# A two-headed attention kernel: input turned by DMA, queries ahead of keys, windowed values made once per token

## The chip, the cores and the metric

The kernel runs on one core of one Trainium2 chip. The metric is the device time of one execution in microseconds; the times shown are those of five executions, and one more view, the profile, comes from one of these five. In the profile's pages PE is TensorE (its weight loads, PEld, are counted apart), ACT is ScalarE, DVE is VectorE, POOL is GpSimd and SP is SyncE, which here only issues DMAs.

## The reference

Two attention blocks with inputs of their own are computed, and their results are laid side by side in the last dimension. Both have 2048 tokens, a width of 448 and 16 heads of 28.

```python
# A: one key head and one value head shared by 16 query heads, every token sees every token
q = (x @ wq).reshape(B, S, 16, 28)      # k = x @ wk, v = x @ wv: 28 columns each
p = softmax(q k^T * 28**-0.5)           # 2048 x 2048 for each head
a = (p @ v).reshape(B, S, 448) @ wo
# B: own keys and values for each head; a token sees 8 tokens: itself, and 2, 4 .. 14 back
q, k, v = split(x @ wqkv)
b = (softmax over those 8) @ v ... @ wo
return concatenate([a, b], axis=-1)
```

A is by far the larger part: 16 x 2048 x 2048 exponentials.

## The kernel before

**A planner writes the order.** `_Gen` runs a small model of the five engines while the program is being built. Each engine has a clock in it (`T`); `loop` takes the engine whose clock is lowest and lets it choose its next step. The order in which steps were chosen is the order in which each engine's instructions stand in the program. Waits on semaphores follow from what each operation reads and writes (`Res`, `emission`). An engine executes its list strictly in order, so a plan that is wrong about a duration shows as a wait in front of whatever stands next. DMA issues stand in the list of the engine that issues them: nearly all on SP, some at the start on ACT, and the weights of B and of the two output projections on POOL.

**Block A.** Scores are made in jobs of 128 keys by 512 queries for one head. A query group is 4 heads by 512 queries (`Group`: 16 key blocks by 4 heads, 64 jobs), and 16 such groups make 1024 jobs. `do_qk` (L1426) issues two or three jobs at once into PSUM banks 0 to 2 or 3 and 4 in turn, and `act_choose` (L1192) takes the exponential of two or three banks with one ACT instruction into one of 8 buffers of `P`. A part of the jobs, called D jobs, does not go through ACT: `dread` makes their exponentials on DVE (L1473), as bit patterns with an offset, with two shifted copies (L1481, L1488, on DVE or POOL), and four small products per job against scaled copies of the values in place of one. `want_d` decides when such a job may be added: among other things the number of finished fills (`nfill`) has to keep up with `FILLN` per 1024 jobs plus `FILL0`, and before 40 us no fill of `x` or `k` may be open. Products with values (`do_pv`, L1536) collect a whole query group in one PSUM bank, four heads at a time.

**Fills.** All else on TensorE is a fill: projections of x into keys, values and queries, norms of the queries, the whole of block B, and the output projections (`outproj`). A fill has a due time and sometimes a condition; `fill_pick` takes the most overdue that can run, `pe_choose` puts it between score jobs where there is room. `dummy` (L1619, L1621) adds products with no use when a running measure of activity falls below `HAMLOW`; `step_ready` holds narrow steps of B back while it is below `HAMTILE`. Both are meant to keep the granted clock up.

**Start of A.** x arrives as 16 blocks of 128 tokens in `xn`, which lies in the upper part of `P`, so only `XFREE` buffers of `P` are free until the last block is turned. Each 512 tokens are transposed on TensorE (L666, four blocks by four pieces of 112 columns, `KA`), and evicted by DVE (L677) or ACT (L675) to `xT_A`. Then come the keys `k0` (L691, evicted at L699), the first query group (L796) with its square on ACT (L825), its copy (L815), a column sum and an addition (L747): a per-query offset that replaces the row maximum. Keys of later chunks and later query groups follow as fills. For B, x is transposed by DMAs on SP (`load_xb`, one after every second exponential).

**Block B.** A token's window reaches at most 14 back, in steps of 2, so even and odd tokens are apart: 4 chunks of 512 tokens, each cut into 21 (`NB`) blocks of 25 queries with 32 keys. Values are projected block by block (L850), 21 products of 4 chunks each, with 7 tokens of each block computed again in the next one, and evicted to `vB` (L857), which has the tokens of chunk c in partitions 32c to 32c+31. Scores (L1269), exponentials (L1290) and products with values (L1231) run for four head groups; a group may start when all values, its keys and its queries are there.

**Ends.** `chain` brings denominators through DRAM (`den`, `rec_scratch`, `bc`: three DMA steps on SP per group), multiplies on POOL (L1006), and `outproj` projects 128 tokens at a time and writes them out.

Of the kernel before, what the change touches and what calls it, by code (L numbers as in the profile page):

```python
# [5 lines left out]
ACT = mybir.ActivationFunctionType  # L6
# [6 lines left out]
S = 2048  # L13
D = 448
H = 16
DH = 28
KA = 112
# [12 lines left out]
HALO = 7  # L30

# [19 lines left out]
T0 = 13.0  # L51
AHEAD = 2
BT0 = 83
BDT = 39
# [20 lines left out]
XFREE = 3  # L75
# [3 lines left out]
HAMLOW = 0.6  # L79
HAMTILE = 0.5  # L80
# [8 lines left out]
XE1 = False  # L89
FILLN = 140.0  # L90
FILL0 = 6.0
# [98 lines left out]
class _Gen:  # L190
# [233 lines left out]
    def alloc(self, es):  # L424
# [7 lines left out]
        self.rec_dram = nc.dram_tensor("rec_scratch", (32, 4, 512), FP32)  # L432

# [42 lines left out]
        self.xn = self.P[:, self.NP * 1536 - 16 * D:].rearrange("p (b c) -> p b c", c=D)  # L476
# [7 lines left out]
    def plan_start(self):  # L484
# [20 lines left out]
        def wA(q, t, src, c1, key, lands):  # L505
            self.dma_op(q, t[0:KA, :, 0:c1], src.rearrange("(k p) c -> p k c", p=KA), writes=[res(key)], lands=lands, name=key)

        def xA(q, c, b0, b1, lands):
            self.dma_op(q, g.xn[:, 4 * c + b0:4 * c + b1, :], g.A_x[0, 512 * c:512 * c + 512, :].rearrange("(p b) c -> p b c", b=4)[:, b0:b1, :],
                        writes=[res("xn", c)] if b0 == 0 else (), appends=[res("xn", c)] if b0 else (), lands=lands, name="x")  # L510
        xA("sp", 0, 0, 2, XL0)
        xA("act", 0, 2, 4, XL0)
        wA("sp", g.wq, g.A_wq, D, "wq", 5000.0)
        wA("act", g.wk, g.A_wk, DH, "wk", 3500.0)
        wA("act", g.wv, g.A_wv, DH, "wv", 4000.0)
        for c in range(1, 4):
            xA("sp", c, 0, 4, 5000.0 + 700 * c)
        dve(lambda e: e.memset(g.zero, 0.0), 100, writes=[res("zero")])
        dve(lambda e: e.memset(g.wk[:, :, DH:32], 0.0), 80, writes=[res("wk0")])
        dve(lambda e: e.memset(g.wv[:, :, DH:32], 0.0), 80, writes=[res("wv0")])  # L520
        dve(lambda e: e.memset(g.wq[:, :, D:456], 0.0), 100, writes=[res("wq0")])
# [39 lines left out]
        gp(lambda e: e.memset(g.vB[:, :, :, DH:32], 0.0), 1400, writes=[res("vB0")])  # L561
        gp(lambda e: e.memset(g.vB[:, :, :, DH:DH + 1], 1.0), 600, reads=[res("vB0")], writes=[res("vB1")])
# [83 lines left out]
    def make_fills(self):  # L646
# [10 lines left out]
        for c in range(4):  # L657
            for kt in (range(4) if c == 0 else (0, 2)):
                n = 1 if c == 0 else 2

                def steps(bank, c=c, kt=kt, n=n):
                    out = []
                    for k in range(n):
                        for b in range(4):
                            x0 = bank * 1024 + 512 * k + 128 * b
                            out.append(("full", lambda e, b=b, k=k, x0=x0: e.transpose(g.psb[0:KA, x0:x0 + 128], g.xn[:, 4 * c + b, KA * (kt + k):KA * (kt + k) + KA],  # L666
                                                                                   g.ident[:, :]), 60.0, [res("xn", c), res("id")]))
                    return out

                def after(bank, c=c, kt=kt, n=n):  # L670
                    src = g.psb[0:KA, bank.i * 1024: bank.i * 1024 + 512 * n].rearrange("p (k t) -> p k t", k=n)
                    dst = g.xT_A[0:KA, kt:kt + n, 512 * c:512 * c + 512]
                    wr = [res("xA", c, kt + k) for k in range(n)]
                    if kt == 3 or (c == 1 and kt == 2):
# [6 lines left out]
                    if sum(self.xdone) == 16:  # L681
                        for k in range(XFREE, self.NP):
                            self.pslots.give(k)
# [164 lines left out]
        for b in range(NB):  # L848
# [5 lines left out]
            def after(bank, b=b):  # L854
                def cb(o):
                    self.vready += 1
# [872 lines left out]
```

## Time and profile before

| | us |
|---|---|
| median of five runs | 412.44 |
| lowest, highest | 410.13, 417.66 |
| the profiled execution, its span | 417.66, 415.8 |
| busy: PE, ACT, DVE, POOL | 402.7, 390.0, 349.9, 114.7 |
| exponentials of A on ACT (L1192), 352 instructions | 377.3 |
| first exponential begins | 12.15 |
| granted TensorE clock, mean | 0.974 |

The busy time of an engine covers the instructions that compute; DMA issues and waits are not in it. Busy shares are means over stages that differ: the start up to 14 us, the long middle, the B groups spread through it, and the last 14 us of output projections. The profiled execution is the longest of the five, and its clock row has a dip that the prediction comes back to.

### The profile page before, as it was taken

How to read it: one execution, taken by the hardware profiler on the slowest of the kernel's cores; microseconds unless marked ns; L12 is line 12 of the kernel's file. 1: busy time of each engine (PE TensorE's matmuls, PEld its weight loads, DVE VectorE, ACT ScalarE, POOL GpSimd, SP SyncE). 2: the span in 40 equal slices, each digit the busy share in tenths (PEclk: the TensorE clock that was granted, in tenths of full speed). 3: DMA queues.
4: the chain of work that ended last, by engine and by line, in shares of the span. 5: the costliest groups of instructions: out<-in, count | busy, mean ns of one | idle time of the engine just before them, and what ended most of it. 6: DMA issues, size and time to landing. Idle time of an engine off the chain costs nothing.

```text
span 415.8 us, 16682 instructions
## 1 busy us (share of the span) xinstructions
PE 402.7 (97%) x7348; PEld 140.9 (34%) x7348; DVE 349.9 (84%) x803; ACT 390.0 (94%) x382; POOL 114.7 (28%) x143
## 2 busy tenths in 40 slices
PE   7999999999999999999999999999999999999996
PEld 3432232322233323334324433233433223444343
DVE  2879999999999999998988998989882398599953
ACT  3899999999999999999999999999996799999972
POOL 8851051202011530404363223414121030110420
PEclk9999999999999999999999999999985699999999
DMA  7099311000010101000221102210011131102415
GB/s 220 20 208 119 68 36 28 4 5 27 2 28 2 30 24 29 6 15 21 54 62 53 29 9 67 66 19 16 6 31 32 29 82 36 43 15 76 105 56 159
DMA packets 31235, 20.15 MB, mean 48 GB/s; under 512 B 21404, under 2 KB 26316, under 8 KB 31164
## 3 DMA queue, kind: packets, MB, share of 16 engines
q1 hardware_dynamic: 29068, 16.37, 16.5%
q0 software_dynamic: 736, 2.20, 3.0%
q8 instruction: 58, 0.95, 1.0%
q10 hardware_dynamic: 1360, 0.51, 0.5%
q14 instruction: 13, 0.11, 0.1%
HBM read 12.42 MB, written 3.92 MB: 39 GB/s over the span
## 4 chain that ended last, share of the span: by engine, by line
ACT 76%; PE 21%; DMA 1%; DVE 1%; issue 0%; ACTq 0%; DVEq 0%
ACT P L1192 74%; PE ps L642 7%; PE ps L1536 6%; PE ps L1426 6%; ACT P L1290 1%; DMA wk<-in_A_wk_dram 1%; PE ps L1231 1%; PE ps L1619 1%; PE ps L1269 1%; PE ps L1259 0%; DVE qT_A L815 0%; PE ps L666 0%; DVE qT_A L747 0%; PE ps L1621 0%; DVE sq L1060 0%
## 5 line engine op out<-in xcount | busy, mean ns | idle before, releaser
L1192 ACT ACTIVATE P<-ps 128x1536 bf16<-128x1536 f32 (+1 forms) x352 | 377.3, 1253 | 7.2 <-PE ps L1426 6.9
L1473 DVE TENSOR_SCALAR Z<-ps 128x512 int16<-128x512 f32 x205 | 139.0, 683 | 15.9 <-PE ps L1426 14.8
L1536 PE MATMUL ps<-P,vA 128*32 128x512 bf16 x819 | 148.1, 394 | 1.0 <-ACT P L1192 0.5
L1426 PE MATMUL ps<-qT_A,kT_A 29*128 29x512 bf16 x1024 | 140.8, 391 | 4.1 <-ACT P L1192 1.8
L1536 PE MATMUL ps<-Z,vA 128*32 128x512 bf16 x820 | 142.9, 389 | 1.2 <-ACT P L1192 0.9
L1488 DVE TENSOR_SCALAR Z<-Z 128x1024 int16<-128x1024 int16 x174 | 77.7, 457 | 1.3
L1426 PEld LDWEIGHTS ps<-qT_A,kT_A 29*128 29x128 bf16 x1024 | 35.5, 91 | 126.8 <-ACT P L1192 65.5
L1006 POOL TENSOR_TENSOR oTn<-PVs,bc 128x512 bf16<-128x512 f32 x15 | 19.1, 1273 | 140.6 <-DVE Z L1481 83.7
L1481 DVE TENSOR_SCALAR Z<-Z 128x512 int16<-128x512 int16 x174 | 49.5, 304 | 1.0
L1536 PEld LDWEIGHTS ps<-P,vA 128*32 128x32 bf16 x819 | 36.2, 94 | 34.0 <-issue 21.3
L1536 PEld LDWEIGHTS ps<-Z,vA 128*32 128x32 bf16 x820 | 35.3, 94 | 35.2 <-issue 22.4
L1481 POOL TENSOR_SCALAR Z<-Z 128x512 int16<-128x512 int16 x31 | 19.1, 617 | 86.0 <-DVE Z L1481 31.8
L642 PE MATMUL ps<-xT_B,wB 128*32 128x512 bf16 x512 | 40.8, 391 | 0.1
L1488 POOL TENSOR_SCALAR Z<-Z 128x1024 int16<-128x1024 int16 x31 | 32.5, 1048 | 5.6 <-DVE Z L1488 3.7
L1006 POOL TENSOR_TENSOR oTnB<-PVs,bc 128x512 bf16<-128x512 f32 x16 | 20.3, 1274 | 47.1 <-DVE Z L1488 26.8
L960 DVE COPY PVs<-ps 128x512 f32<-128x512 f32 x31 | 21.2, 684 | 12.8 <-PE ps L1231 10.5
L642 PE MATMUL ps<-wB,xT_B 128*32 128x448 bf16 x336 | 24.5, 354 | 0.0
L642 PE MATMUL ps<-xT_A,wq 112*32 112x512 bf16 x256 | 20.3, 383 | 0.3 <-DVE qT_A L815 0.3
L642 PE MATMUL ps<-woA,oTn 128*32 128x448 bf16 x256 | 17.6, 356 | 0.0
L1060 DVE CAST sq<-ps 128x448 bf16<-128x448 f32 x15 | 9.2, 622 | 8.6 <-PE ps L642 8.1
L642 PEld LDWEIGHTS ps<-xT_B,wB 128*32 128x32 bf16 x512 | 10.6, 96 | 14.8 <-issue 8.9
L1231 PE MATMUL ps<-P,vB 32*32 32x25 bf16 (+1 forms) x1344 | 15.2, 173 | 0.0
(96 smaller groups left out, 271.0 us busy)
## 6 DMA issues: line engine op xcount, KB each, us to landing
bc<-rec_scratch SPq DMA_DIRECT2D x124, 64.0 KB, 2.1
out_dram<-sq SPq DMA_DIRECT2D x17, 112.0 KB, 1.8
out_dram<-ob SPq DMA_DIRECT2D x13, 112.0 KB, 1.7
P<-in_A_x_dram SPq DMA_DIRECT2D x3, 448.0 KB, 7.0
wB<-in_B_wqkv_dram POOLq DMA_DIRECT2D x1, 1008.0 KB, 6.1
den<-PVs SPq DMA_DIRECT2D x31, 8.0 KB
rec_scratch<-rec SPq DMA_DIRECT2D x31, 8.0 KB, 1.7
wq<-in_A_wq_dram SPq DMA_DIRECT2D x1, 392.0 KB, 5.5
```

What stands on the lines that cost most here:

```text
L642: ins = e.matmul(self.bank(bank, 32 * j, 32 * j + m, 0, n), lhs(j), rhs(j), start=start, stop=stop, tile_position=(0, 32 * j))
L960: return dict(emit=lambda e: e.tensor_copy(out=g.PVs[:, p, :], in_=g.bank(bank.i)), reads=[bank.res], writes=[self.pvs.res[p]], took=ns + ...
L1006: return dict(emit=lambda e: e.tensor_tensor(out=dst(z), in0=g.PVs[:, p, :], in1=g.bc[:, b, :], op=ALU.mult), reads=[self.pvs.res[p], self ...
L1060: em = lambda e: e.tensor_copy(out=self.obuf[o_], in_=g.bank(bank.i, 0, 128, 0, D))
L1192: op = self.put("act", lambda e: e.activation(g.P[:, 1536 * k:1536 * k + 512 * n], g.ps[:, lo:lo + 512 * n], ACT.Exp, scale=ASCALE), ns, n ...
L1231: ins = e.matmul(g.bank(bank, 32 * j, 32 * j + 32, q0, n), g.vB[32 * c:32 * c + 32, b, 4 * gg + j, :], g.P[32 * c:32 * c + 32, x:x + n], s ...
L1269: ins = e.matmul(g.bank(bank, 32 * c, 32 * c + 32, q0, n), g.kT_B[32 * j:32 * j + DH + 1, s, k0:k0 + 32], g.qT_B[32 * j:32 * j + DH + 1, s ...
L1426: ins = e.matmul(g.bank(b), g.kT_A[32 * j:32 * j + DH + 1, 128 * tb:128 * tb + 128], g.qT_A[32 * j:32 * j + DH + 1, gr.sc % 2, gr.g, :], s ...
L1473: return dict(emit=lambda e: e.tensor_scalar(out=g.Z[:, z, 0, :], in0=g.bank(bank.i), scalar1=ZBIAS, scalar2=0.0, op0=ALU.add, op1=ALU.max ...
L1481: return dict(emit=lambda e: e.tensor_scalar(out=g.Z[:, z, 1, :], in0=g.Z[:, z, 0, :], scalar1=1.0, scalar2=32.0, op0=ALU.mult, op1=ALU.ad ...
L1488: return dict(emit=lambda e: e.tensor_scalar(out=g.Z[:, z, 2:4, :], in0=g.Z[:, z, 0:2, :], scalar1=1.0, scalar2=64.0, op0=ALU.mult, op1=AL ...
L1536: ins = e.matmul(g.bank(b, 32 * j, 32 * j + 32), l, r, start=st, stop=sp, tile_position=(0, 32 * j))
```

## The change

- The contraction of A is cut into three pieces of 128 columns and a fourth that covers the last 128 again, with the weights' upper 64 rows set to zero there (`KA` is 128, `x0`). Each weight of A is loaded with two DMAs.
- Only the first 512 tokens go through `xn` and TensorE. The other three chunks are written to `xT_A` by twelve DMA transposes on SP, issued right after the first loads. wq's load moves to ACT's queue, wk's to SP's. A key fill of a later chunk is open once its last piece is due by the plan.
- The first query group stands before the first keys, and its copy on DVE has a higher priority.
- Values of B are projected once per token: 16 products of 128 tokens, evicted to four stages that share the second half of `kT_B`, stored to a DRAM scratch (16 DMAs), and read back in blocks, two or three DMAs per chunk (`v_blocks`, ten in all). The second head group of B waits until all ten are counted.
- Constants of the planner: T0 13 to 9, BT0 83 to 98, BDT 39 to 36, XFREE 3 to 6, HAMLOW 0.6 to 0.7, HAMTILE 0.5 to 0.55, FILLN 140 to 130, FILL0 6 to 0.

```diff
-KA = 112
+KA = 128
+def x0(kt):
+    return 128 * kt if kt < 3 else D - 128
...
-T0 = 13.0
+T0 = 9.0
-BT0 = 83
-BDT = 39
+BT0 = 98
+BDT = 36
-XFREE = 3
+XFREE = 6
-HAMLOW = 0.6
-HAMTILE = 0.5
+HAMLOW = 0.7
+HAMTILE = 0.55
-FILLN = 140.0
-FILL0 = 6.0
+FILLN = 130.0
+FILL0 = 0.0
...
+        self.v_dram = nc.dram_tensor("v_scratch", (S, H * 32), BF16)
+        self.vst = self.kT_B[:, 1, :].rearrange("p (v h d) -> p v h d", h=H, d=32)
...
-        wA("sp", g.wq, g.A_wq, D, "wq", 5000.0)
-        wA("act", g.wk, g.A_wk, DH, "wk", 3500.0)
+        wA("act", g.wq, g.A_wq, D, "wq", 3800.0)
+        wA("sp", g.wk, g.A_wk, DH, "wk", 4000.0)
         for c in range(1, 4):
-            xA("sp", c, 0, 4, 5000.0 + 700 * c)
+            for kt in range(4):
+                self.dma_op("sp", g.xT_A[:, kt, 512 * c:512 * c + 512], g.A_x[0, 512 * c:512 * c + 512, x0(kt):x0(kt) + 128], writes=[res("xA", c, kt)],
+                            transpose=True, issue=1310.0, lands=3000.0, moves=1200.0, name="xAt")
...
-            fill(f"k{c}", (-84, T0 - 1, T0 + 3, T0 + 8)[c], steps, after, ring=True)
+            fill(f"k{c}", (-84, T0 + 1, T0 + 5, T0 + 10)[c], steps, after, ring=True, enabled=landed if c else None)
...
-                due = (-85 if gg == 0 else T0 - 12 + 18 * gg) if sc == 0 else -40 + gg
+                due = (-90 if gg == 0 else T0 - 12 + 18 * gg) if sc == 0 else -40 + gg
...
-        for b in range(NB):
+        for b in range(16):
             def steps(bank, b=b):
-                return [("col", self.proj4(bank, lambda j, kt=kt: g.xT_B[:, kt, 512 * j + bk0(b, j % 2):512 * j + bk0(b, j % 2) + 32],
+                return [("col", self.proj4(bank, lambda j, kt=kt: g.xT_B[:, kt, 128 * b + 32 * j:128 * b + 32 * j + 32],
...
+                            return dict(dma=True, out=g.v_dram[128 * b:128 * b + 128, :], in_=g.vst[:, k, :, :].rearrange("p h d -> p (h d)"),
+                                        reads=[self.vsts.res[k], res("vB1")], writes=[res("vd", b)], lands=2600.0, moves=500.0, cb=cb)
...
+    def v_blocks(self, c):
+        vd = [res("vd", b) for b in range(max(0, 4 * c - 1), 4 * c + 4)]
+        h = c % 2
+        for b0, n in ((0, 1), (1, NB - 2), (NB - 1, 1)) if h == 0 else ((0, NB - 1), (NB - 1, 1)):
+            src = g.v_dram[512 * c + bk0(b0, h):512 * c + bk0(b0, h) + 32, :]
+            if n > 1:
+                src = bass.AP(src.tensor, src.offset, [[H * 32, 32], [BQ * H * 32, n], [1, H * 32]])
...
+                out = g.vB[32 * c:32 * c + 32, b0:b0 + n, :, :].rearrange("p b h d -> p b (h d)")
+            self.later(("sp",), (560 if n == 1 else 900,), vd, mk, prio=2.5, name="vb")
...
-            if self.q0done and self.nnorm == 0 and f.name not in ("qn0.0", "x1.0"):
+            if self.q0done and self.nnorm == 0 and f.name not in ("qn0.0", "k0"):
```

## The prediction

> **What bounds the kernel now.** I read the page first: busy shares, the row of the granted clock, the chain that ended last. Lines of the page:
>
> ```profile
> PE 402.7 (97%) x7348; PEld 140.9 (34%) x7348; DVE 349.9 (84%) x803; ACT 390.0 (94%) x382; POOL 114.7 (28%) x143
> ...
> PEclk9999999999999999999999999999985699999999
> ...
> ACT 76%; PE 21%; DMA 1%; DVE 1%; issue 0%; ACTq 0%; DVEq 0%
> ```
>
> Three engines are nearly full at once. ScalarE (the exponentials) carries the chain, TensorE the rest of it, and for a while near 310 us the clock fell to about half. So I asked for busy time by stretch; columns are the stretch, then each engine's busy us with its instruction count, the granted clock, DMA share and GB/s:
>
> ```profile
> 20.00:30.00 10.00, 9.35 (x127) 3.18 (x125) 7.55 (x23) 10.00 (x10) 6.79 (x12) 1.00 1.03 204
> ...
> 100.00:120.00 20.00, 19.60 (x261) 5.87 (x265) 18.91 (x46) 20.00 (x20) 1.46 (x2) 1.00 0.06 16
> ...
> 220.00:240.00 20.00, 20.00 (x565) 8.27 (x558) 18.31 (x45) 20.00 (x23) 5.20 (x5) 1.00 0.14 39
> ...
> 310.00:330.00 20.00, 20.00 (x339) 5.35 (x332) 5.95 (x14) 13.76 (x13) 1.27 (x1) 0.51 0.13 32
> ...
> 402.00:416.00 14.00, 10.09 (x210) 5.44 (x208) 6.53 (x11) 4.24 (x8) 0.00 (x0) 0.96 0.43 133
> ```
>
> From 20 us to the clock's fall ScalarE hardly rests: in the middle the time is set by how many exponentials it is given. VectorE takes about a fifth of them (the D jobs: 205 of 1024), and TensorE, full too, feeds both. At 310 to 330 the clock of 0.51 starves ScalarE of 6.2 us; with 0.13 and 0.25 us in the two stretches ahead this profile lost 6.6 us. The end is 14 us of output projections. The profiled execution took 417.66 us (span 415.8 and 1.86 around it); less 6.6 it would be 411.0, one of the five runs shown is 411.04, and their median is 412.44. So I sum changes on an undisturbed profile and apply the difference to the median, which keeps 1.4 us of disturbance.
>
> The start, from the timeline (start us, duration, engine, line, what, idle before and releaser):
>
> ```profile
> 7.10 0.61 PE L642 MATMUL ps<-xT_A,wk 112*32 112x512 bf16 x8 [0.66 <-DMA wk<-in_A_wk_dram]
> ...
> 8.38 1.04 PE L642 MATMUL ps<-xT_A,wq 112*32 112x512 bf16 x16
> ...
> 9.47 0.60 ACT L825 ACTIVATE sq<-ps 128x512 bf16<-128x512 f32 x1 [0.17 <-PE ps L642]
> ...
> 10.96 0.69 DVE L747 TENSOR_TENSOR qT_A<-ps,qT_A 128x512 bf16<-128x512 f32 x1
> ...
> 12.15 1.45 ACT L1192 ACTIVATE P<-ps 128x1536 bf16<-128x1536 f32 x1
> ...
> 14.16 2.37 ACT L1192 ACTIVATE P<-ps 128x1024 bf16<-128x1024 f32 x2 [0.56 <-PE ps L1426]
> ```
>
> Keys go first on TensorE, queries second, though the query has the longer way: square, column sum, add, score. And the groups by line (busy us, mean ns):
>
> ```profile
> L1192 ACT ACTIVATE P<-ps 128x1536 bf16<-128x1536 f32 (+1 forms) x352 | 377.3, 1253 | 7.2 <-PE ps L1426 6.9
> ...
> L1473 DVE TENSOR_SCALAR Z<-ps 128x512 int16<-128x512 f32 x205 | 139.0, 683 | 15.9 <-PE ps L1426 14.8
> ...
> L1488 DVE TENSOR_SCALAR Z<-Z 128x1024 int16<-128x1024 int16 x174 | 77.7, 457 | 1.3
> ...
> L1481 DVE TENSOR_SCALAR Z<-Z 128x512 int16<-128x512 int16 x174 | 49.5, 304 | 1.0
> ...
> L857 DVE CAST vB<-ps 128x448 bf16<-128x448 f32 x21 | 13.0, 618 | 0.6 <-PE ps L642 0.6
> ...
> L677 DVE COPY xT_A<-ps 112x1024 bf16<-112x1024 bf16 (+1 forms) x8 | 4.5, 585 | 3.7 <-PE ps L666 3.7
> ```
>
> An A job costs ScalarE 377.3/819 = 0.461 us. A D job costs VectorE 0.683 + 0.304 + 0.457 = 1.444 us, and TensorE three more small products (820 of Z for 205 jobs), about 0.16 us at 0.22 us per four in the chain.
>
> **The change, part by part.**
>
> *Start.* The query product would no longer stand behind 1.28 us of key product (7.10 to 8.38). With the last transposed piece there at 7.08 and wq at 6.8 (issued 1.26, 5.5 us to landing), the first exponential moves from 12.15 to between 10.4 and 10.9. Keys then run on TensorE while ScalarE squares; their copy, 0.69 us on ScalarE, ends before the query's add on VectorE does. The gap of 0.56 ahead of 14.16 comes from TensorE doing the second chunk's 512 tokens between scores, which goes too in part. The value is 1.3 to 2.2; I take 1.8. What is late next is wq: it now stands behind x on ScalarE's DMA queue, as it stood behind x on SP's. Each A weight becomes two DMAs, so ScalarE issues five at about 0.45 instead of three: its table load slips 0.9, against 2.7 us of idling ahead of its first copy at 6.48, so nothing. The new zeroing on VectorE is three memsets of 0.1, hidden likewise in its first 5 us. The contraction's 128 rows instead of 112 cost nothing (380 ns for xT_B,wB at 128 rows, 383 for xT_A,wq at 112).
>
> *Tokens beyond 512 by DMA.* Removed: 48 TensorE transposes, 0.60 to 0.66 us per eight, 3.8 us; five VectorE copies of 0.687, 3.4 us; one ScalarE copy of 1.02, which ended as the first exponential's input was ready. Added: 12 DMA transposes on SP. The nearest rows are B's own:
>
> ```profile
> xT_B<-in_B_x_dram SPq DMA_TRANSPOSE x16, 4.8
> ...
> wq<-in_A_wq_dram SPq DMA_DIRECT2D x1, 392.0 KB, 5.5
> ...
> wk<-in_A_wk_dram ACTq DMA_DIRECT2D x1, 24.5 KB, 5.7
> ```
>
> Each occupies SP for 1.13 us and lands after 2.7 to 6.8 (4.8 in the middle). SP has x and two wk pieces ahead, so they issue from 2.2 us: the second chunk is issued by 6.7 and lands at 8.3 to 12.4, the third 4.5 us later, the fourth by 22 at worst. When are they needed? The first chunk holds 16 jobs in query group 0 and 16 in group 1. At 0.46 us per job and a start at 10.5, group 0 lasts until about 18. Slack 5 us and more: I cost it at nothing. If that cover is gone, TensorE stands in its queue at the second chunk's key product with all scores behind it. Behind them on SP wait B's transposes, which began at 17.47; the last A issue is at about 16, so they hardly move.
> Here the Trainium skill speaks against the change: "VectorE: DVE Perf Modes", its section on the three transpose paths, gives 1309 ns for a 128x128 block by DMA and 390 on TensorE, and its rules prefer TensorE when PSUM will do. By that price, four blocks to a DMA and one after another, a chunk takes 16 x 1.31 = 21 us and lands at 23, 44 and 65. The rows (four blocks in 1.13 us of issue, 128 KB moving in about a microsecond at 47 to 50 us) make it a fifth. I take the rows, as the same operation on the same queue, and keep the page's price for a rival.
>
> *B's values once per token.* Removed: 5 of 21 products of 16 matmuls, 0.75 us each (rows of 16 with woB, 448 columns as well), 3.8 us; five evictions of 0.618, 3.1 us. Added on SP: 16 stores of 128 KB and 10 block loads, 26 issues of about 0.45 (bc 0.42), 12 us of SP, idle for most of these 100 us. The four large loads move some 0.6 MB each: by wB's 1008 KB in 6.1 us, 3.9 us each; if a quarter of the partitions means a quarter of the rate, 16. Between them 16 to 64 us in all; I take the near row. Values were complete at 128 us and first wanted after 175, when B's first exponential runs; even 64 us from the last store near 90 is hidden. The denominators' DMAs stand behind these on SP: in that stretch a chain runs every 22 to 25 us with four PVs buffers, so 16 us of delay costs nothing; less cover would hold a PSUM bank. The stage shares the second half of B's keys, so the second head group's keys wait for all ten loads; they are wanted at 225. Smaller POOL memsets and six P buffers instead of three free nothing that waits.
>
> *Pace and clock.* D jobs began at 24.87, once all fills of x and k were issued; the DMA version allows them from about 20. VectorE idled 2.4 us from 20 to 30, gets 6.5 back, and has more room after 180. The pace rule is lower: at the end up to 151 - 130 = 21 fills may remain instead of 162 - 146 = 16 (14 blocks did remain), five blocks of 0.75, 3.8 us of tail. So gains pass through two limits. TensorE: 3.8 + 3.8 less 0.16 per extra D job. ScalarE: 1.8 + 0.461 per extra D job, less whatever tail grows. Three extra jobs (VectorE's freed 6.5 us with losses) to 14 (its spare room too) are possible; I take 8, 11.6 us of VectorE, from 6.5 freed and about 5 of room: 3.7 us on ScalarE, and TensorE nets 6.3, which pays for it and part of the tail. Sum 1.8 + 3.7 = 5.5.
> The clock: "TensorE: Matmul & The Clock Gate", Part 1, has the array slow after an idle window of about 3.4 us, in a free-running window. Here it fell at 308 with TensorE busy 9.83 of 10 us, amid runs of 25-column products. By the page this loss could not happen; by the trace narrow work suffices, 6.6 us when it does. Thresholds of 0.7 and 0.55 put in more filler and hold narrow products back: 0 to 1.4 off the median, or the 6.6 once more; I take 0.
>
> **Forecast:** 412.44 - 5.5 = 406.9, say 407 (404.5 to 409.5), chance 0.48.
>
> **Rivals.**
> *Only the start counts*, 0.23: extra D jobs are eaten by five blocks more in the tail, 412.4 - 1.8 - 3.7 + 3.8 = 410.7, up to 415 if fillers or a clock drop add. For it: the tail follows the pace rule already. Against: TensorE does have 7.6 us less to do.
> *TensorE is the true bound*, 0.14: all 7.6 us plus the start's 1.8 come through, 403; with the disturbance gone, 401.6. For: B's fills run far behind their due times (values due by 66, done at 128). Against: VectorE must find 13 more jobs.
> *Transposes late*, slower, 0.13: if a transpose takes over 3.8 us, (17.5 - 2.2)/4, the second chunk misses the end of group 0's jobs and TensorE's queue stands. At the page's price, group 1 stretching each chunk to 32 jobs or 15 us, ScalarE waits about 5 + 6 + 6 = 17 us: 412.4 - 5.5 + 17 = 424; at half of that, 417.
> *It doesn't do what it says*, 0.02: values wait for DRAM until B's groups move behind 200; 415.
>
> **Numbers.** One per cent, 4 us, is about what five runs spread over 7.5 us can tell from no change. Below 408.3 lie 0.14 and some 0.44 of the forecast's; above 416.6 the late transposes and a little of the first rival, 0.14; the rest 0.28. The range, 402 to 414.5, leaves out the late transposes and the extremes.
>
> **What would show it.** First exponential at 10.4 to 10.9; no wait of TensorE on xT_A's DMA; last of 12 transposes landed by 22; 16 rows instead of 21 for B's value copy; Z conversions 208 to 219; ScalarE's last exponential about 5 to 8 us earlier and a tail up to 4 longer. I am wrong if ScalarE idles at 15 to 40 us, if the count of D jobs stays, or if the clock row dips for longer.

## The result and the profile after

| | before | after |
|---|---|---|
| median of the compared runs, us | 410.77 | 407.73 |
| the profiled execution, its span | 417.66, 415.8 | 404.94, 403.2 |
| first exponential begins, last one ends | 12.15, 400.69 | 10.19, 390.60 |
| from there to the end of the span | 15.1 | 12.6 |
| exponentials of A on ScalarE, busy | 377.3 | 371.7 |
| D jobs on VectorE | 205 | 215 |

The ratio is 0.9907 (0.9889 to 0.9925): nine tenths of a per cent shorter, a little inside the one per cent that the prediction drew as its line. The median of before rests on 62 runs here and not on five, and lies 1.7 us lower than the five showed: the dip of the clock in its profiled execution is missing from most of its runs (of 28 that ran beside the first four experiments, 20 have a mean clock of 0.998 and more). Ratios, here and below, are made of the executions within 1.5% of the fastest of their kernel, medians of all.

Three rows of the page of the kernel after:

```profile
PE 386.6 (96%) x7281; PEld 135.0 (33%) x7281; DVE 346.5 (86%) x803; ACT 384.1 (95%) x371; POOL 129.8 (32%) x165
...
PEclk9979999999999999999999999999999999999999
...
ACT 74%; PE 15%; SPq 4%; DVE 4%; DMA 2%; issue 0%
```

TensorE is busy 16 us less (part of what it was busy before was the slow clock) and VectorE does ten more D jobs. The dip near 310 us is gone, a small one is there in the third slice, and the chain that ended last now has SP's queue (SPq) and a DMA in it, which it lacked before. The windows (stretch, then busy us and instructions of PE, PEld, DVE, ACT, POOL, granted clock, DMA share, GB/s) say what that cost:

```profile
20.00:30.00 10.00, 7.58 (x86) 1.96 (x88) 5.81 (x17) 6.63 (x7) 4.30 (x8) 0.75 1.13 193
30.00:40.00 10.00, 9.89 (x125) 2.72 (x120) 8.94 (x24) 9.56 (x9) 0.00 (x0) 0.91 1.19 142
```

ScalarE, 10.00 of 10 in both before and now, lacks 3.4 and 0.4 us. The timeline of that stretch names it (start, duration, engine, line, what, idle before and its releaser):

```profile
17.23 6.88 ACT L1214 ACTIVATE P<-ps 128x1536 bf16<-128x1536 f32 x6 [0.16 <-PE ps L1467]
...
18.18 1.35 POOL L324 DMA_DIRECT2D wB<-in_B_wqkv_dram  x2
...
19.17 11.73 SPq L324 DMA_TRANSPOSE xT_B<-in_B_x_dram  x5
...
22.41 0.40 PE L654 MATMUL ps<-xT_A,wk 128*32 128x512 bf16 x4
...
25.22 0.62 PE L654 MATMUL ps<-xT_A,wk 128*32 128x512 bf16 x4 [2.41 <-DMA xT_A<-in_A_x_dram]
...
26.20 0.61 PE L1467 MATMUL ps<-qT_A,kT_A 29*128 29x512 bf16 x3
...
26.86 2.37 ACT L1214 ACTIVATE P<-ps 128x1536 bf16<-128x1536 f32 x2 [2.74 <-PE ps L1467]
```

The key product of the fourth chunk stands at the head of TensorE's list, with three of its four pieces done, and waits 2.41 us for the last of the twelve transposes. All scores stand behind it, so ScalarE waits 2.74. When TensorE goes on, the same matmul takes 0.62 us that took 0.40 at 22. Read in steps of a microsecond, the granted clock is 0.50 from 25 to 31 us; the first and the last of these steps:

```profile
25.00:26.00 1.00, 0.78 (x8) 0.14 (x8) 0.11 (x1) 0.00 (x0) 0.58 (x1) 0.50 1.44 146
...
30.00:31.00 1.00, 1.00 (x11) 0.16 (x3) 0.74 (x2) 1.00 (x1) 0.00 (x0) 0.50 0.84 79
```

The chain of waits shows the transfer itself (start, duration, what):

```profile
16.56 1.26 SPq L324
17.82 0.04 issue
17.86 7.31 DMA xT_A<-in_A_x_dram
25.18 0.04 issue
25.22 0.62 PE ps L654 x4
```

Issued at 17.86, it landed 7.3 us later, next to B's weights (issued from 18.18), the output weights (from 19.50) and B's transposes (from 19.17).

The start went as drawn. On the timeline, two lines:

```profile
6.38 1.05 PE L654 MATMUL ps<-xT_A,wq 128*32 128x512 bf16 x16 [0.54 <-DMA wq<-in_A_wq_dram]
...
7.25 1.04 PE L654 MATMUL ps<-xT_A,wk 128*32 128x512 bf16 x16
```

Queries first, keys second, what is late is wq. And the groups by line (busy us, mean ns, idle before):

```profile
L1214 ACT ACTIVATE P<-ps 128x1536 bf16<-128x1536 f32 (+1 forms) x341 | 371.7, 1275 | 5.6 <-PE ps L1467 5.5
L1514 DVE TENSOR_SCALAR Z<-ps 128x512 int16<-128x512 f32 x215 | 146.6, 685 | 21.2 <-PE ps L1467 19.8
...
L876 DVE CAST kT_B<-ps 128x448 bf16<-128x448 f32 x16 | 9.9, 618 | 3.2 <-PE ps L654 3.2
```

**Where the time went, by the two profiled executions.** The span fell by 12.6 us: first exponential 1.96 earlier; ScalarE busy 5.4 us less between the first exponential and the last (381.4 to 376.0; ten fewer A jobs are 4.6 of it, the rest goes with 341 instructions where there were 352); idle in between 4.5 for 7.2; the end 2.5 shorter. Before, 6.6 of the 7.2 idle was the clock's dip. Against an execution without it, 411.0, the change saved some 6, and idle time rose by 3.9, nearly all of it the 3.8 at 20 to 40 us. The question for the runs was therefore not where a gain had gone, but what the wait at 23 us costs, why it is there, and whether the prediction was right for its own reasons.

### The profile page after: what moved, and what is told of

Its sections match the earlier page's. It is cut to its first block, busy times and chain, and to the rows that moved or that the text cites. A ratio compares the mean times of both kernels' runs of the same rounds, so it can differ in the third digit from the quotient of the medians.

```text
span 403.2 us, 16636 instructions
## 1 busy us (share of the span) xinstructions
PE 386.6 (96%) x7281; PEld 135.0 (33%) x7281; DVE 346.5 (86%) x803; ACT 384.1 (95%) x371; POOL 129.8 (32%) x165
## 4 chain that ended last, share of the span: by engine, by line
ACT 74%; PE 15%; SPq 4%; DVE 4%; DMA 2%; issue 0%
ACT P L1214 73%; PE ps L1577 5%; SPq L324 4%; PE ps L1467 4%; PE ps L654 3%; DMA xT_A<-in_A_x_dram 2%; DVE Z L1514 2%; ACT P L1331 1%; PE ps L1310 1%; PE ps L1272 1%; DVE Z L1529 1%; PE ps L1300 0%; DVE sq L1082 0%; PE ps L1660 0%; DVE Z L1522 0%
## 5 line engine op out<-in xcount | busy, mean ns | idle before, releaser
L1214 ACT ACTIVATE P<-ps 128x1536 bf16<-128x1536 f32 (+1 forms) x341 | 371.7, 1275 | 5.6 <-PE ps L1467 5.5
L1514 DVE TENSOR_SCALAR Z<-ps 128x512 int16<-128x512 f32 x215 | 146.6, 685 | 21.2 <-PE ps L1467 19.8
L1577 PE MATMUL ps<-P,vA 128*32 128x512 bf16 x809 | 140.0, 389 | 1.0 <-ACT P L1214 0.8
L1467 PE MATMUL ps<-qT_A,kT_A 29*128 29x512 bf16 x1024 | 135.0, 387 | 4.5 <-ACT P L1214 1.9
L1522 POOL TENSOR_SCALAR Z<-Z 128x512 int16<-128x512 int16 x42 | 26.1, 624 | 90.6 <-DVE Z L1514 50.9
L1529 POOL TENSOR_SCALAR Z<-Z 128x1024 int16<-128x1024 int16 x42 | 43.9, 1047 | 7.7 <-DVE Z L1529 4.0
L654 PE MATMUL ps<-xT_A,wq 128*32 128x512 bf16 x256 | 19.5, 383 | 0.7 <-DMA wq<-in_A_wq_dram 0.5
L654 PE MATMUL ps<-wB,xT_B 128*32 128x448 bf16 x256 | 18.1, 355 | 0.1
L654 PE MATMUL ps<-woB,oTnB 128*32 128x448 bf16 x256 | 15.2, 353 | 0.0
L1310 PE MATMUL ps<-qT_B,kT_B 29*32 29x25 bf16 (+1 forms) x1344 | 14.7, 173 | 0.0
```

Of the source, the lines that this page charges most:

```text
L654: ins = e.matmul(self.bank(bank, 32 * j, 32 * j + m, 0, n), lhs(j), rhs(j), start=start, stop=stop, tile_position=(0, 32 * j))
L1214: op = self.put("act", lambda e: e.activation(g.P[:, 1536 * k:1536 * k + 512 * n], g.ps[:, lo:lo + 512 * n], ACT.Exp, scale=ASCALE), ns, n ...
L1310: ins = e.matmul(g.bank(bank, 32 * c, 32 * c + 32, q0, n), g.kT_B[32 * j:32 * j + DH + 1, s, k0:k0 + 32], g.qT_B[32 * j:32 * j + DH + 1, s ...
L1467: ins = e.matmul(g.bank(b), g.kT_A[32 * j:32 * j + DH + 1, 128 * tb:128 * tb + 128], g.qT_A[32 * j:32 * j + DH + 1, gr.sc % 2, gr.g, :], s ...
L1514: return dict(emit=lambda e: e.tensor_scalar(out=g.Z[:, z, 0, :], in0=g.bank(bank.i), scalar1=ZBIAS, scalar2=0.0, op0=ALU.add, op1=ALU.max ...
L1522: return dict(emit=lambda e: e.tensor_scalar(out=g.Z[:, z, 1, :], in0=g.Z[:, z, 0, :], scalar1=1.0, scalar2=32.0, op0=ALU.mult, op1=ALU.ad ...
```

## The experiments

Two theories. **Mine:** the last transpose lands late because B's loads crowd the DMA engines, and this wait, with the half clock behind it, eats a gain larger than the one I forecast. **The rivals:** the transposes are slow on their own account; or the plan is at fault, since it assumes 3.0 us for a landing and puts the product where it must wait; or the wait costs no more than its 2.4 us, and the modest gain is all that the freed work gives. A ratio is to the kernel before, with its 95% interval.

**The same orders, B's weights later.** The two loads of `wB` and the output weights stay on POOL in their order, but behind the eviction of the fourth chunk's keys. No other instruction of POOL stood between, so the engines' orders are those of the kernel after; in the two traces SP, VectorE, ScalarE and GpSimd have the same instructions in the same order.

```diff
     def emission(self):
+        k3 = [o for o in self.ops if o.name == "ke"][3]
+        w = [o for o in self.ops if o.name == "w" and o.idx < k3.idx]
...
+        self.ops = [o for o in self.ops if o not in w]
+        i = self.ops.index(k3) + 1
+        self.ops[i:i] = w
...
+        w[0].deps.append(k3)
```

> The changed kernel with every engine's order of instructions kept; only the load of B's weights on POOL (wB, and the output weights behind it) waits until the fourth chunk's keys of A are evicted. Theory (the 1 MB of wB delays the last of A's DMA transposes, which took 7.3 us to land, and TensorE's queue stands 2.4 us at the fourth key product and then runs at half clock to 31 us): that wait shrinks to under 0.5 us, the last transpose lands in under 4 us, the clock row has no dip at 25 to 31, ScalarE idles under 1 us at 20 to 32 instead of 3.8, and the total falls by 2.5 to 4 us, to 403 to 405 (somewhat less if the first product with wB then waits for it). Rival (A's last transpose is held up by B's transposes queued on SP or by the transposes' own rate): wait, dip and time stay as they are, 407 to 408.

Measured: 402.17 us (401.67 to 402.34), ratio 0.978 (0.9745 to 0.9816). The timeline of this kernel (its lines are ten further down):

```profile
23.14 0.40 PE L664 MATMUL ps<-xT_A,wk 128*32 128x512 bf16 x4 [0.31 <-DMA xT_A<-in_A_x_dram]
...
24.64 1.33 POOL L324 DMA_DIRECT2D wB<-in_B_wqkv_dram  x2 [6.43 <-DVE Z L1532]
```

Its windows:

```profile
20.00:30.00 10.00, 9.26 (x127) 2.92 (x128) 8.43 (x25) 9.88 (x9) 5.06 (x8) 1.00 0.67 168
30.00:40.00 10.00, 9.50 (x125) 2.69 (x121) 8.07 (x19) 10.00 (x10) 1.25 (x2) 1.00 1.18 109
```

The last transpose landed after 5.5 us, more than the 4 I had expected, but 2.1 earlier on the clock of the span; the wait is 0.31, the clock stays 1.00, and ScalarE gets back 3.7 of its 3.8 us there. By the last exponential 2.6 of them are left, since 1.1 us of idle time stands elsewhere, and the profiled executions differ by 2.75. In the medians it is 5.6 (5.2 by the ratios), and the runs lie within 0.7 us of each other where those of the kernel after are spread over 6.0. The wait costs about 2.7 us in one execution and about twice that in the middle of many.

The clock, which is on record for every execution, says where the slower ones lose it. In all six of this kernel its mean is 0.997 or more; in all 31 of the kernel after that count for the ratio it lies between 0.983 and 0.996. The 13 of these at 0.993 and above have a median of 405.3 us, the 8 at 0.987 and below 408.5. So the slower executions are those with more slow clock. That it stands behind the wait is seen only in the profiled one, where it is the only dip; why it lasts longer in some, and whether the wait is longer in them too, no profile here shows.

**The crowd from the other side.** `wB` stays in place; B's transposes begin after the 14th exponential and not the third. The order is planned anew.

```diff
-self.nexp >= 3 and
+self.nexp >= 14 and
```

> The changed kernel with B's input transposes on SP starting after 14 exponentials in place of 3; the plan is the same up to the fourth key product. Theory (wB is what delays A's last transpose): the landing stays above 6 us and TensorE's wait of 2.4 us stays; total 406 to 409, B's values starting later. Rival (B's transposes on the same queue delay it): landing under 4 us, wait under 0.5 us, no clock dip, total 403 to 405.

405.86 us (404.54 to 409.72), ratio 0.9893 (0.9858 to 0.9928).

```profile
23.18 0.40 PE L654 MATMUL ps<-xT_A,wk 128*32 128x512 bf16 x4 [0.30 <-DMA xT_A<-in_A_x_dram]
```

The wait is 0.30 us, the landing 5.46, ScalarE busy 9.88 and 10.00 in the two stretches, the clock 1.00 in both. So the theory that `wB` alone delays the transpose failed: it stayed where it was, and the wait went. Of the rival's signs the wait and the clock came true, the landing under 4 us and the total of 403 to 405 did not. Taking either load out of the crowd removes the wait. The total did not follow, since this is another plan: the exponentials end at 385.20, earlier than in the first experiment (387.98), and the end takes 18.8 us where it took 12.5.

**The plan told the truth.** The last four transposes are entered with 7.3 us to landing instead of 3.0.

```diff
-transpose=True, issue=1310.0, lands=3000.0, moves=1200.0, name="xAt")
+transpose=True, issue=1310.0, lands=3000.0 if c < 3 else 7300.0, moves=1200.0, name="xAt")
```

> The changed kernel whose plan is told a landing of 7.3 us for the four transposes of the last chunk, so that the fourth key product stands later in TensorE's list; no transfer is moved. Theory (the loss is one of order: keys of the fourth chunk are not needed before about 50 us, and the product merely stands too early in TensorE's list): no wait on the DMA over 0.5 us, no dip of the clock, total 403 to 405.5, a little of it given back because D jobs start later. Rival (keys of that chunk are really needed by then): ScalarE idles all the same, total 407 or more.

418.61 us (413.69 to 430.66), ratio 1.0131 (1.0066 to 1.0197): slower than either kernel. Windows and timeline of it:

```profile
20.00:30.00 10.00, 9.94 (x151) 3.27 (x149) 5.96 (x17) 10.00 (x10) 3.73 (x7) 1.00 1.09 180
30.00:40.00 10.00, 5.24 (x55) 1.27 (x51) 3.53 (x13) 4.35 (x5) 0.61 (x1) 0.83 1.30 97
```

```profile
18.25 1.35 POOL L324 DMA_DIRECT2D wB<-in_B_wqkv_dram  x2
...
26.05 0.40 PE L654 MATMUL ps<-xT_A,wk 128*32 128x512 bf16 x4
...
34.03 0.37 PE L654 MATMUL ps<-wB,xT_B 128*32 128x448 bf16 x4 [2.24 <-DMA xT_B<-in_B_x_dram]
...
38.88 2.37 ACT L1214 ACTIVATE P<-ps 128x1536 bf16<-128x1536 f32 x2 [5.65 <-PE ps L1467]
```

This answers one thing cleanly: the last piece of the fourth chunk's key product runs at 26.05, later than the 25.22 of the kernel after, and ScalarE is full at 20 to 30 us all the same. So those keys were not needed yet; only their place in TensorE's list made them urgent. And it shows the same fault one step on. Now the first product of B's values stands at the head of the list and waits, piece after piece, for transposes that landed after 13.7 us in the middle (7.1 in the kernel after, counted over the same stretch from 18 to 40 us). To correct one duration in the plan moves the wait to the next one that is too short. It isn't the whole of the loss: the exponentials end 3.5 us later than in the kernel after, and the end takes 22.9 us where that took 12.6, which belongs to the new plan.

The trace also limits what the crowd explains. `wB` is issued here at 18.25 and B's transposes begin at 18.62, much as in the kernel after (18.18 and 19.17), and still A's last transpose landed 5.2 us after its issue, and not 7.3:

```profile
xT_A<-in_A_x_dram SPq DMA_TRANSPOSE x1, 5.2
```

It had left at 17.31, 0.9 us ahead of `wB`; in the kernel after it was 0.3. So holding back a load removes the wait, but that the crowd alone makes 7.3 us is not shown; how much hangs on who starts first, no run here separates.

**More of the crowd out of the way.** The first experiment again, with the output weights held until the last of B's transposes.

```diff
-        w = [o for o in self.ops if o.name == "w" and o.idx < k3.idx]
...
+        w = [o for o in self.ops if o.name == "w"]
...
-        self.ops[i:i] = w
+        self.ops[i:i] = w[:2]
+        i = max(n for n, o in enumerate(self.ops) if o.name == "xBt") + 1
+        x = self.ops[i - 1]
+        self.ops[i:i] = w[2:]
...
+        w[2].deps.append(x)
```

> The kernel of e1_wb_waits, the output weights' loads besides held back until the last of B's transposes is issued; all other orders kept. Theory (the DMAs between 20 and 40 us are crowded, which is what makes whatever transfer is planned tightest land late): B's transposes land sooner, no wait of TensorE on a DMA after 20 us over 0.3 us, total 401 to 402.2 with runs within 1 us. Rival (wB alone was the trouble): the same 402.2 within 0.4 us.

401.89 us (401.59 to 403.95), ratio 0.9798 (0.9778 to 0.9819). B's transposes land in 4.3 us instead of 5.5 (the median of all 16), and the time is that of the first experiment within 0.3, which both sides had in their range; the runs lie within 2.4 us and not within 1. Once the wait is gone, a thinner crowd buys nothing that these runs can tell.

**One part at a time, on the kernel before.** Queries first, with wq's and wk's loads exchanged and the first query's copy ahead of other work on VectorE:

```diff
-        wA("sp", g.wq, g.A_wq, D, "wq", 5000.0)
-        wA("act", g.wk, g.A_wk, DH, "wk", 3500.0)
+        wA("act", g.wq, g.A_wq, D, "wq", 3800.0)
+        wA("sp", g.wk, g.A_wk, DH, "wk", 4000.0)
...
-                due = (-85 if gg == 0 else T0 - 12 + 18 * gg) if sc == 0 else -40 + gg
+                due = (-90 if gg == 0 else T0 - 12 + 18 * gg) if sc == 0 else -40 + gg
```

> The kernel before with one part of the change: first queries ahead of first keys, with wq and wk on exchanged DMA queues. Theory: the first exponential starts at 10.4 to 10.9 instead of 12.15 and the total falls by 1 to 2 us, to 408.5 to 409.8 against 410.8. Rival (a start gained is lost again, since the keys of the second chunk and the other fills are not there sooner): ScalarE idles between 12 and 20 us by as much, total 410 to 411.

412.86 us (410.14 to 415.78), ratio 1.0066 (1.0038 to 1.0094). The first exponential begins at 12.09, where it was. The timeline says why:

```profile
11.17 1.02 ACT L675 ACTIVATE xT_A<-ps 112x1024 bf16<-112x1024 bf16 x1 [0.58 <-PE ps L666]
...
11.29 0.39 PE L1424 MATMUL ps<-qT_A,kT_A 29*128 29x512 bf16 x3
...
12.09 3.70 ACT L1190 ACTIVATE P<-ps 128x1536 bf16<-128x1536 f32 x3
```

The score is ready at about 11.7, but ScalarE is still copying the second chunk out of PSUM. That copy goes only with the DMA transposes. The longer median goes with the clock: of the 17 executions, six have a mean clock of 0.999 and more and take 410.14 to 412.37, the other eleven, at 0.990 to 0.996, take 412.27 to 415.78. Why this kernel meets the slow clock more often than the kernel before stays open.

Values once per token alone: the 16 products, the stores, the block loads and the conditions that depend on them, with the constants of before.

```diff
-        for b in range(NB):
+        for b in range(16):
...
-            fill(f"vB{b}", BT0 - 65 + 2.4 * b, steps, after, elig=30.0)
+            fill(f"vB{b}", BT0 - 62 + 2.4 * b, steps, after, elig=30.0)
...
-            en = lambda gg=gg: gg < 2 or self.b_issued >= 4 * (gg - 1)
+            en = lambda gg=gg: gg == 0 or (self.vready == 10 if gg == 1 else self.b_issued >= 4 * (gg - 1))
```

> The kernel before with one part of the change: B's values made once per token and brought into blocks through DRAM, the planner's constants as before. Theory (3.8 us of TensorE and 3.1 us of VectorE are freed and turned into D jobs at 0.46 us of ScalarE each, at most): total 0.5 to 2.5 us under the kernel before, 408 to 410.3 against 410.8, with 205 to 209 Z conversions. Rival (26 more DMAs on SP delay the denominators or B's first group): POOL and VectorE wait for bc and den, total 411 to 414.

407.65 us (406.31 to 415.71), ratio 0.9933 (0.9907 to 0.996), a little better than the 408 to 410.3 of the theory, with 207 D jobs and no wait for the trip through DRAM (POOL waits 11.7 us for the denominators' last step, 13.1 in the kernel before). This is the part that gains by itself.

The DMA transposes alone, with the cut of the contraction into pieces of 128 and six buffers of `P`, keys still first:

```diff
-            xA("sp", c, 0, 4, 5000.0 + 700 * c)
+            for kt in range(4):
+                self.dma_op("sp", g.xT_A[:, kt, 512 * c:512 * c + 512], g.A_x[0, 512 * c:512 * c + 512, x0(kt):x0(kt) + 128], writes=[res("xA", c, kt)],
+                            transpose=True, issue=1310.0, lands=3000.0, moves=1200.0, name="xAt")
```

> The kernel before with one part of the change: A's tokens beyond 512 turned by DMA (with the 128-row cut of the contraction and six P buffers), keys still first, constants as before. Theory: TensorE is freed of 3.8 us, VectorE of 3.4, the first exponential no longer stands behind ScalarE's 1.02 us copy of the second chunk and starts at 11 to 11.7; but with wB's load next to the last transposes, TensorE waits 0.3 to 3 us for xT_A as in the changed kernel, and times of single runs spread over 4 us or more; total 407 to 410.5. Rival (the transposes are free of cost): no wait on xT_A over 0.3 us in the profile, runs within 2 us, total 405 to 407.

418.05 us (416.53 to 420.75), ratio 1.0196 (1.0161 to 1.0231). Both totals missed, and the wait on `xT_A` that the theory had is not there: with `wB` issued only at 20.34, the last of these transposes landed after 4.6 us. Its windows, timeline and groups:

```profile
20.00:30.00 10.00, 9.46 (x140) 2.98 (x134) 8.67 (x27) 10.00 (x10) 6.41 (x11) 1.00 1.08 202
30.00:40.00 10.00, 6.70 (x70) 1.67 (x67) 6.61 (x18) 6.17 (x6) 0.00 (x0) 0.85 1.17 101
```

```profile
37.07 0.62 PE L654 MATMUL ps<-xT_B,wB 128*32 128x512 bf16 x4 [2.06 <-DMA xT_B<-in_B_x_dram]
...
38.29 2.37 ACT L1202 ACTIVATE P<-ps 128x1536 bf16<-128x1536 f32 x2 [3.83 <-PE ps L1436]
```

```profile
L1483 DVE TENSOR_SCALAR Z<-ps 128x512 int16<-128x512 f32 x192 | 130.7, 683 | 20.1 <-PE ps L1436 19.1
```

The wait is on B's transposes here, 3.0 us of TensorE in two pieces and 3.8 of ScalarE at 30 to 40. And 13 D jobs are missing. The likely reason is the pace rule: there are six fills fewer than before to finish, while `FILLN` and `FILL0` still ask for as many, so `want_d` says no more often. At 0.461 us each the 13 are 6.0 us of ScalarE. No run sets the rule anew in this kernel, so its share of the 7.6 us isn't measured; and the count of fills is not all of it, since the values alone took five fills away and left 207 D jobs.

The three ratios multiply to 1.020; together, with the new constants, they make 0.9907. The parts don't add.

**The constants.** The first experiment with the old pace, planned anew:

```diff
-FILLN = 130.0
-FILL0 = 0.0
+FILLN = 140.0
+FILL0 = 6.0
```

> The kernel of e1_wb_waits (wB's load held back) with the pace of D jobs as before: FILLN 140 and FILL0 6. Theory (the lower pace lets ScalarE have fewer jobs): 6 to 12 fewer Z conversions than its 215, ScalarE's last exponential 2 to 4 us later, a tail shorter by up to 3.8 us, total within 2 us above e1_wb_waits' 402.2. Rival (the pace rule doesn't bind): the number of conversions stays at 213 or more and the total within 0.7 us.

405.21 us (403.25 to 408.96), ratio 0.989 (0.9849 to 0.9932): 203 D jobs for 215, the last exponential at 393.70 for 387.98, the end 9.3 us for 12.5. The pace does trade the middle for the end, and the trade is good, but probably by less than the 3 us between the medians: a line of its timeline and its window,

```profile
34.06 0.94 PE L664 MATMUL ps<-wB,xT_B 128*32 128x448 bf16 x16 [2.12 <-DMA wB<-in_B_wqkv_dram]
```

```profile
30.00:40.00 10.00, 7.85 (x108) 2.33 (x101) 6.81 (x17) 7.99 (x9) 1.25 (x2) 1.00 1.17 119
```

show a wait that the first experiment lacks, and ScalarE is busy only 7.99 of 10 us there. Of the 2.6 us between the profiled executions that may be 2.0. The clock stays 1.00 behind this wait.

The first experiment with the old thresholds, planned anew too:

```diff
-HAMLOW = 0.7
-HAMTILE = 0.55
+HAMLOW = 0.6
+HAMTILE = 0.5
```

> The kernel of e1_wb_waits with the thresholds of filler products as before: HAMLOW 0.6 and HAMTILE 0.5. Theory (the thresholds keep the clock from falling in B's narrow stages): mean granted clock of single runs falls below 0.99 in some of them, their times spread to 406 or more, median 402.5 to 405. Rival (with the wait on the DMA gone nothing makes the clock fall): fewer filler products than 100, all runs within 1.5 us, median 401 to 402.5.

407.28 us (404.22 to 410.02), ratio 0.9907 (0.9874 to 0.9941), longer than the 402.5 to 405 of the theory. The clock row of its page, one digit for 10.2 us, has a dip of the kind that the kernel before showed:

```profile
PEclk9998999999999999999999999998599999999999
```

Not all of the 5.1 us goes with the clock: the two executions with a mean of 0.997 and 1.000 took 404.22 and 404.28, still 2 us longer than the first experiment. It pointed to the thresholds as a gain of their own. So they went into the kernel before, alone and with the pace:

```diff
-HAMLOW = 0.6
-HAMTILE = 0.5
+HAMLOW = 0.7
+HAMTILE = 0.55
```

> The kernel before with only the two thresholds of the change, HAMLOW 0.7 and HAMTILE 0.55. Theory (they are worth time of their own, since with e1_wb_waits' kernel the old pair cost 5 us): no dip of the clock in the profile, runs within 2 us of each other, median 407 to 409.5 against 410.4. Rival (they only help where the freed TensorE time leaves gaps to fill; in the full kernel before, filler takes room from work): median 410 to 413.

422.32 us (421.64 to 430.46), ratio 1.028 (1.0266 to 1.0294). That theory fell, and the rival's 410 to 413 was too short as well: 228 filler products instead of 68, and 196 D jobs.

```diff
-HAMLOW = 0.6
-HAMTILE = 0.5
-FILLN = 140.0
-FILL0 = 6.0
+HAMLOW = 0.7
+HAMTILE = 0.55
+FILLN = 130.0
+FILL0 = 0.0
```

> The kernel before with the thresholds and the pace of D jobs of the change (FILLN 130, FILL0 0), nothing else. Theory (the pace must fall because there are fewer fills; with all 162 fills a lower pace lets more D jobs in but leaves output projections for the end): 211 to 222 Z conversions instead of 205, the last exponential 2 to 6 us earlier, a tail longer by 2 to 6 us, total within 2 us of e11_clock_alone. Rival (the pace alone was set too high before): total 3 us or more under e11_clock_alone.

410.76 us (409.01 to 412.44), ratio 0.9999 (0.9977 to 1.0021). The groups and the last 20 us of it:

```profile
L1473 DVE TENSOR_SCALAR Z<-ps 128x512 int16<-128x512 f32 x218 | 148.6, 684 | 21.2 <-PE ps L1426 18.9
```

```profile
389.00:409.00 20.00, 15.69 (x321) 8.63 (x317) 9.77 (x16) 4.89 (x10) 3.82 (x3) 1.00 0.48 144
```

It does 218 D jobs, ends its exponentials at 389.11, 11.6 us before those in the profile of the kernel before (6.6 of these are that profile's dip), and then takes 19.7 us to its end, where that took 15.1. I had expected it within 2 us of the thresholds alone; it is 11.6 under them, more than the 3 that the rival asked for; the pace alone, without the thresholds, was not run. These four constants alone move work to the end and gain nothing. With work taken off TensorE the pace did gain (402.17 against 405.21 above); that this is why the earlier end of the exponentials stays a gain there is argued from the two pairs, not shown.

**The better loading order, planned anew.** The planner is told of the late loads (`load_late` runs when the fourth chunk's keys are evicted) and writes a new order:

```diff
-            rd = [res("kA", 0), res("wB0")]
+            rd = [res("kA", 3), res("wB0")]
...
-                           prio=0.5 if c == 0 else 1, name="ke", cb=lambda o: self.load_late(c) if c < 3 else None)
+                           prio=0.5 if c == 0 else 1, name="ke", cb=lambda o: [self.load_late(w) for w in range(3)] if c == 3 else None)
```

> The changed kernel with the weights' loads triggered by the fourth chunk's keys and the whole plan made anew around that. Theory (a later load only costs if products with wB are planned ahead of its landing, and the plan allows 9 us for that): no wait on xT_A over 0.5 us as in e1_wb_waits, but twelve more filler products at 30 us and B's values later; total 402 to 405. Rival (any new plan scatters by more than this effect): 405 or more with no wait on a DMA to explain it.

412.72 us (411.15 to 417.59), ratio 1.0075 (1.0036 to 1.0113). No wait on `xT_A` at the start, a clock of 1.0, 221 D jobs, exponentials that end at 385.14, and an end of 24 us:

```profile
394.79 1.26 POOL L1026 TENSOR_TENSOR oTnB<-PVs,bc 128x512 bf16<-128x512 f32 x1 [5.68 <-DMA bc<-rec_scratch]
...
396.10 3.40 PE L654 MATMUL ps<-woB,oTnB 128*32 128x448 bf16 x68 [1.70 <-POOL oTnB L1026]
...
400.24 1.27 POOL L1026 TENSOR_TENSOR oTnB<-PVs,bc 128x512 bf16<-128x512 f32 x1 [4.20 <-DMA bc<-rec_scratch]
```

The last group of B comes so late that its denominators' way through DRAM is the end of the kernel. The rival came true: the same intention, 10.6 us apart from the first experiment by the order that the planner happened to find. A run that plans anew tells what that plan costs; an effect by itself is measured only where the order stays.

## Why the prediction was right, and where not

The time, 407.73 against 407, and the range held. The difference, 3.0 us against 5.5, did not, since the median of before was 1.7 us lower than the five runs showed; and two of the terms were wrong in opposite directions: with the wait removed the change is worth 8.6 us by the medians, and the wait takes 5.6 of them. That 407 came out so closely is luck.

- **The start, 1.8:** right. 1.96, first exponential at 10.19, 0.2 ahead of the window of 10.4 to 10.9; wq is what is late, as said. One execution of each is a loose measure: in the four profiled kernels with the old start it begins at 11.66 to 12.54, in the eight with the new one at 10.06 to 10.82. What I did not see is that neither part gives it alone: 12.09 with queries first, where ScalarE's copy of 1.02 us is next in line, and 11.63 with DMA transposes and keys first.
- **The DMA transposes, "Slack 5 us and more: I cost it at nothing":** this step failed, twice. The landing "by 22 at worst" was 25.2: an issue took 1.26 us in the middle and one of them 2.28, where B's row gave 1.13, so the last one left at 17.9 and not at 16, and it took 7.3 us, beyond the 6.8 that was the longest in the trace of before, in the stretch into which I had moved it and in which B's loads run. And I counted the need by when ScalarE runs out of jobs. It is set by where the product stands in TensorE's list. The sentence that followed, "If that cover is gone, TensorE stands in its queue at the second chunk's key product with all scores behind it", described the mechanism; it was the fourth chunk's. Cost: 2.7 us in the profiled executions, 5.6 in the medians, for a term that stood at zero. The rival *Transposes late* had this mechanism, at the second chunk and with 17 us (half of which makes 415.4 by its sum, not 417); it said slower, and the kernel got faster, since the wait was 2.4 us and came once.
- **Row against page:** the three transpose paths of "VectorE: DVE Perf Modes" in the Trainium skill make an estimate of 63 us for 48 blocks of 1309 ns one after another. The twelve were issued from 2.35 and landed by 25.2. The row was the right choice for the size; neither told how long a landing takes beside B's loads.
- **Values once, 3.8 of TensorE and 3.1 of VectorE, the trip hidden:** right; alone it gives 0.9933. The loads of 640 KB into 32 partitions landed in 5.9 us, between the two ends of 3.9 and 16. They were wanted sooner than I wrote: B's first exponential stands at 118.9 and not behind 175. The last load, issued at 93.66, landed in 2.9 us, and the first product that reads the values runs at 137.3, so some 40 us of cover were left.
- **Pace, eight more D jobs or 3.7 us:** ten, and 5.4 us less of ScalarE between the first and last exponential. The end did not grow but shrank by 2.5, where I allowed up to 4 more. This term was sized too small; with the wait removed the sum is 402.2, which is the number of "TensorE is the true bound" (403, or 401.6 undisturbed), a rival to which I gave 0.14. It came by ten jobs and a shorter end, not by the 13 jobs that I held against it; that TensorE is what bounds the kernel, no run shows.
- **The clock, "I take 0":** the dip near 310 is gone from this profile, but a new one of 6 us follows the wait. And "by the trace narrow work suffices" was read from one execution: the same products run in every execution of the kernel before, and most of these show no dip (20 of 28 at 0.998 and more), so narrow work alone doesn't decide it; what does stays open. What the thresholds alone are worth is not settled: taking them back from the first experiment costs 5.1 us, putting them into the kernel before costs 11.6, and the plans differ in both.
- **"I am wrong if ScalarE idles at 15 to 40 us":** it does, 3.8 us. The total stood because the gain was larger.

Still open beside the thresholds: what makes the slow clock more frequent with queries first alone, why it lasts longer in some executions of the kernel after than in others, and how much of the late landing is the crowd and how much who starts first in it.

## What to carry to other kernels

On an engine that executes in order, the deadline of a transfer is the place of its first reader in that engine's list, not the moment at which the result is wanted; so cost a moved transfer by its landing in the stretch it is moved into, with everything that loads there. Where a planner or a pacing rule writes the order, test a cause with the order held fixed: here one loading order gave 402.2 us in the old order and 412.7 in a new one. And when work is removed, look for the rules that may count it.

## What the runs showed of the hardware

- DMA transposes of 128 by 512 took SP 1.26 us each for A's input (one took 2.28) and 1.13 for B's once the start was over; in the crowd from 19 to 33 us of the kernel after, B's took 1.3 to 3.4. From issue to landing A's took 2.8 us (issued at 15.26, before `wB`) to 7.3 (issued at 17.86), and B's 13.7 in the middle between 18 and 40 us of the run with the told plan (DMA share 1.30 at 30 to 40: the time of the packets was 1.3 times that of the 16 engines).
- The granted clock fell to 0.50 after TensorE had stood for 2.41 us, and stayed there for 6 us in which TensorE was nearly full; with a wait of 0.31 us it did not fall, and with one of 2.12, in the run with the old pace, it did not fall either. The Trainium skill, "TensorE: Matmul & The Clock Gate", Part 1, has an idle window of about 3.4 us ahead of that; here less was enough.
- Stores of 128 KB to DRAM landed in 3.1 us and block loads of 640 KB into 32 partitions in 5.9, nearly the time that `wB`'s 1008 KB took in the same kernel (6.6): a quarter of the partitions did not mean a quarter of the rate.

```profile
v_scratch<-kT_B SPq DMA_DIRECT2D x16, 128.0 KB, 3.1
...
vB<-v_scratch SPq DMA_DIRECT2D x2, 640.0 KB, 5.9
...
wB<-in_B_wqkv_dram POOLq DMA_DIRECT2D x1, 1008.0 KB, 6.6
```
